# Reordering a kernel's start, its side jobs and the PSUM banks of its tail: attention plus token-mixing MLP on one core

## Chip, cores, metric

One core of a Trainium2 chip. The metric is the device time of one execution in microseconds (us), median of the executions. "Span" is the time from the first to the last profiled instruction; in these runs a timed execution is 1.7 us longer than its span. All comparisons are between executions of the fast state.

## The reference, cut to what matters

```python
xn = layernorm(x)                         # 2048 tokens x 1024
out = x + A(xn, wq, wk, wv, wo, beta) + B(xn, w1, b1, w2, b2)
# A: 32 heads of 32, 4 segments of 512 tokens: causal softmax attention inside a segment, plus
#    a linear-attention memory of the earlier segments, mixed by sigmoid(beta); then @ wo
# B: h = layernorm(xn); u = gelu(h^T w1 + b1) over tokens; y = u w2 + b2; transposed back
```

## The kernel before

One instruction stream per engine, written in program order by Python; semaphores are put in where data or PSUM banks are shared. It runs in four stages: the norm of the tokens with the first 512 hidden units (`h`, `w1early`), the rest of the MLP (a seven-product block scheme), 32 attention units (4 segments x 8 groups of 4 heads), and a tail. These parts are touched.

Names in the profile. `h` is a normed chunk of the MLP's input, `xs` the scaled tokens of a later segment. `kT` is the copy of the keys and `ost` that of the weighed values out of PSUM, the banks into which TensorE writes its products; a bank is free for the next product only when its copy is done. `pT` is the exp of the logits, on ScalarE. `srec`, `prod` and `o_s` scale a unit's output by its denominators and add its two parts; `fin` adds a product with `wo` to the output.

The start. `D`/`d` are a chunk's statistics on VectorE (a quote is the second half), `A` on ScalarE, `S` the reciprocal root (one VectorE and one GpSimd instruction), `h` the scaling that makes `h`:

```python
for kind, c0, n in (("x", 0, 1), ("x", 1, 1), ("x", 2, 1), ("w", 0, 2), ("x", 3, 1), ("x", 4, 2), ("w", 2, 2), ("x", 6, 2),
                    ("w", 4, 4), ("x", 8, 4), ("w", 8, 4), ("x", 12, 4), ("w", 12, 4)):
    ...                                   # one DMA each, chunks c0 to c0 + n of x or of w1's first 512 columns
for _ in range(self.N_WARM):              # N_WARM = 12
    fw.mm(self.bank(0), self.warm[:, 0:P], self.warm[:], start=True, stop=True)

NORM_ORDER = (["D0 A1 S0 d2 h0 A1' A3 S1 d2' h1"] +
              [f"S{c} d{c + 2} h{c} A{c + 1}' A{c + 3} S{c + 1} d{c + 2}' h{c + 1}" for c in range(2, 14, 2)] +
              ["S14 h14 A15' S15 C h15"])
```

The attention. TensorE's matmuls are cut into pieces (`dense`), and between the pieces one "side" job at a time is taken from a queue and emitted, mostly for VectorE. How many jobs a unit puts into the queue decides between which matmul pieces each of them falls, and so its place among VectorE's other instructions:

```python
def products(half):                       # combine(): scale a unit's outputs by their denominators
    n = slice(16 * half, 16 * half + 16)
    fw.op("dve", lambda e: e.tensor_tensor(self.prod[:, n, :], ost[:, n, 0:D_HEAD],
                                           rec[:, n].unsqueeze(2).to_broadcast([P, 16, D_HEAD]), op=ALU.mult), ...)
return [scales, lambda: products(0), lambda: products(1), add]        # four side jobs
...
# attention(), per unit u
c = 4 * (u // N_GRP + 1) + u % N_GRP
xn = u % N_GRP < 4 and c < N_TCH          # units 0-3, 8-11, 16-19 scale a chunk of the next segment's tokens
if xn:
    self.xn_load(c)
...
self.side.append(steps.pop(0))            # scales
self.side.append(lambda u=u: self.phi_q(u))
self.side.extend(steps)                   # products, products, add with the transposing DMA
self.side.append(lambda u=u: (self.phi_k(u + 1), self.k_transpose(u + 1)))
if xn:
    self.side.append(lambda c=c: (self.xn_scale(c), self.xn_transpose(c)))
```

`dense` jobs use PSUM banks 6 and 7 in turn, logits banks 0 to 3, the weighing of the values banks 4 and 5. The tail multiplies the last segment's output by `wo`:

```python
i, h, b = n // 2, n % 2, (6, 7, 0, 1, 2, 3, 5, 4)[n]      # bank of tail product n
```

The softmax here doesn't subtract the row's maximum and nothing guards it: scores larger than these inputs give would overflow.

Of the kernel before, what the change touches and what calls it, by code (L numbers as in the profile page):

```python
# [7 lines left out]
ALU = mybir.AluOpType  # L8
# [7 lines left out]
D_HEAD = 32  # L16
# [3 lines left out]
P = 128  # L20
N_TCH = S_TOK // P
# [8 lines left out]
N_GRP = N_HEAD // 4  # L30
# [354 lines left out]
class _Kernel:  # L385
    SB_BASE = 16512
    SB_END = 229344
    LEAD = 2
    N_WARM = 12
    G_AT = 3584  # L390
    B_AT = G_AT + 7 * 14336

# [104 lines left out]
    def consts(self):  # L497
        fw = self.fw
        fw.op("dve", lambda e: e.memset(self.warm[:], 0.0), writes=[self.R_warm])
        for brow, R in ((self.brow1, self.R_brow1), (self.brow2, self.R_brow2)):  # L500
            fw.op("dve", lambda e: e.memset(brow[:], 0.0), writes=[R[4]])
        self.w1_ring = _Ring(fw, [t[:] for t in self.w1s], self.R_w1s, depth=0)
        for fp in range(2, N_FCH // 2):
            self.w1_ring.srcs.append(self.B_w1[:, fp * 256:(fp + 1) * 256].rearrange("(c p) f -> p c f", p=P))
        fw.op("act", lambda e: e.activation(self.junk[:, 0:1], self.warm[:, 0:1], ACT.Gelu_apprx_tanh),
              reads=[self.R_warm], writes=[self.R_junk])
        for kind, c0, n in (("x", 0, 1), ("x", 1, 1), ("x", 2, 1), ("w", 0, 2), ("x", 3, 1), ("x", 4, 2), ("w", 2, 2), ("x", 6, 2),
                            ("w", 4, 4), ("x", 8, 4), ("w", 8, 4), ("x", 12, 4), ("w", 12, 4)):
            if kind == "x":
                self.load_x(c0, n)  # L510
            else:
                self.fw.dma(self.w1early[:, c0:c0 + n, :],
                            self.B_w1[c0 * P:(c0 + n) * P, 0:512].rearrange("(c p) f -> p c f", p=P),
                            writes=self.R_w1e[c0:c0 + n])
        for brow, src, n, R in ((self.brow1, self.B_b1, N_FCH, self.R_brow1), (self.brow2, self.B_b2, N_TCH, self.R_brow2)):
            for j in range(4):
                fw.dma(brow[32 * j:32 * j + n, :], src.rearrange("(c q) -> c q", q=P)[:, 32 * j:32 * j + 32],
                       reads=[R[4]], writes=[R[j]])
        fw.dma(self.beta[:], self.A_beta.partition_broadcast(P), writes=[self.R_beta])
        self.w1_ring.ensure(0)  # L520
        self.w1_ring.ensure(1)

        fw.op("pool", lambda e: e.memset(self.expo[:], -0.5), writes=[self.R_expo])
        fw.op("pool", lambda e: e.memset(self.ident[:], 0.0), writes=[self.R_ident])
        fw.op("pool", lambda e: e.affine_select(self.ident[:], self.ident[:], pattern=[[-1, P]],
                                                compare_op=ALU.not_equal, fill=1.0, base=0,
                                                channel_multiplier=1),
              reads=[self.R_ident], writes=[self.R_ident])
        with fw.group(reads=[self.R_warm], writes=[self.R_bank[0]]):
            for _ in range(self.N_WARM):  # L530
                fw.mm(self.bank(0), self.warm[:, 0:P], self.warm[:], start=True, stop=True)
# [13 lines left out]
    def gates(self):  # L545
# [12 lines left out]
        fw.op("dve", lambda e: e.tensor_copy(self.gate[:, :, 1, :], gv),  # L558
              reads=[self.R_gcol, self.R_gate], writes=[self.R_gate])

    NORM_ORDER = (["D0 A1 S0 d2 h0 A1' A3 S1 d2' h1"] +
                  [f"S{c} d{c + 2} h{c} A{c + 1}' A{c + 3} S{c + 1} d{c + 2}' h{c + 1}" for c in range(2, 14, 2)] +
                  ["S14 h14 A15' S15 C h15"])

    def norm_and_first_hidden(self):
        for word in " ".join(self.NORM_ORDER).split():
            kind, second = word[0], word.endswith("'")
            c = int(word[1:].rstrip("'") or 0)
            if kind == "C":
                self.bias_columns()  # L570
            elif kind in "Dd":
                self.stats_dve(c, (0, 1) if kind == "D" else (1,) if second else (0,))
            elif kind == "A":
                self.stats_act(c, second)
            elif kind == "S":
                self.rstd(c)
            else:
                self.scale_h(c)
        for c in range(N_TCH - 2):
            self.early_hidden(c, c + 1, (range(0, 8, 2), range(1, 8, 2)))  # L580
        self.early_hidden(N_TCH - 2, N_TCH, [(b,) for b in range(8)])
        self.rstd_first()
# [37 lines left out]
        fw.op("pool", lambda e: e.tensor_tensor(rs, rs, self.expo[:], op=ALU.pow), reads=[self.R_rs0, self.R_expo],  # L620
              writes=[self.R_rs0])

    def scale_h(self, c):
        reads = [self.R_xin[c], self.R_st[c], self.R_rs[c]]
        both = getattr(self, f"h_{c % 2}")
        for h0, h1 in ((0, 1), (1, 2)) if c < 2 else ((0, 2),):
            src = self.xin[:, c, 512 * h0:512 * h1].rearrange("p (d x) -> p d x", x=512)
            self.fw.op("dve", lambda e: e.tensor_scalar(both[:, h0:h1, c // 2, :], src, self.ln_mv[:, c, 0:1],
                                                        self.ln_rs[:, c, 1:2], op0=ALU.subtract, op1=ALU.mult),
                       reads=reads, writes=[self.R_h[c % 2][d][c // 2] for d in range(h0, h1)])  # L630
# [649 lines left out]
    def combine(self, u):  # L1280

        fw = self.fw
        s, g, o = u // N_GRP, u % N_GRP, u % 2
        ost, R_ost = self.ost[o], self.R_ost[o]
        rec, R_rec = self.srec[:, o, :], self.R_srec[o]
# [23 lines left out]
            fw.op("dve", lambda e: e.reciprocal(rec, rec), reads=[R_rec], writes=[R_rec])  # L1309
            fw.op("dve", lambda e: e.tensor_tensor(rv, rv, g8, op=ALU.mult), reads=[R_rec, self.R_gate], writes=[R_rec])  # L1310

        def products(half):
            n = slice(16 * half, 16 * half + 16)
            fw.op("dve", lambda e: e.tensor_tensor(self.prod[:, n, :], ost[:, n, 0:D_HEAD],  # L1314
                                                   rec[:, n].unsqueeze(2).to_broadcast([P, 16, D_HEAD]), op=ALU.mult),
                  reads=R_ost + [R_rec, self.R_prod], writes=[self.R_prod])

        def add():
            pv = self.prod[:].rearrange("p (q k r) d -> p q k (r d)", q=4, k=2)
# [2 lines left out]

        if s == 0:
            return [scales_first, products_first]
        return [scales, lambda: products(0), lambda: products(1), add]

    def o_transpose_dma(self, u):
        s, g, o = u // N_GRP, u % N_GRP, u % 2
# [12 lines left out]
              reads=[self.R_bank[b]], writes=[self.R_oT[s % 2][g]])  # L1341

    STOPS, STOPS_DVE = (1, 4, 7), (1, 4)

    def unit_jobs(self, u):
        jobs = [self.wo_job(*x) for x in self.wo_plan.get(u, ())]
# [7 lines left out]
    def attention(self):  # L1354
# [17 lines left out]
        for u in range(N_UNIT):  # L1372
            even = u % 2 == 0
            self.jobs.extend(self.unit_jobs(u))
            total = 8 * len(self.jobs) - sum(j[0] for j in self.jobs)
            c = 4 * (u // N_GRP + 1) + u % N_GRP
            xn = u % N_GRP < 4 and c < N_TCH
            if xn:
                self.xn_load(c)
            if u < 10:  # L1380
                cuts = self.cut(total, (0, 4, 2, 4, 1, 13, 8) if even else (7, 3, 2, 4, 1, 15))
            else:
                cuts = self.cut(total, (0, 4, 2, 2, 2, 14, 8) if even else (7, 3, 2, 2, 2, 16))
            end = u >= N_UNIT - 4
            self.dense(cuts[0])
            self.logits(u, 0)
            self.dense(cuts[1], end)
            while end and self.side:
                self.side.popleft()()
            if u:  # L1390
                self.weigh(u - 1, 0)
            self.dense(cuts[2], False)
            if u:
                self.weigh(u - 1, 1)
            self.dense(cuts[3], False)
            if u:
                self.weigh(u - 1, 2)
                steps = self.combine(u - 1)
                last = steps[-1]
                steps[-1] = lambda u=u, last=last: (last(), self.o_transpose_dma(u - 1))  # L1400
                self.side.append(steps.pop(0))
            if N_GRP <= u:
                self.side.append(lambda u=u: self.phi_q(u))
            if u:
                self.side.extend(steps)
            if u + 1 < N_UNIT:
                self.side.append(lambda u=u: (self.phi_k(u + 1), self.k_transpose(u + 1)))
            if xn:
                self.side.append(lambda c=c: (self.xn_scale(c), self.xn_transpose(c)))
            self.dense(cuts[4])  # L1410
            self.logits(u, 1)
            if even:
                self.dense(cuts[5])
                self.logits(u, 2)
            self.dense(100)
# [13 lines left out]
    def tail(self):  # L1429
        fw = self.fw  # L1430
        s, u = N_SEG - 1, N_UNIT - 1
# [2 lines left out]
            self.load_fin(4 * s + i)  # L1434

        def product(n, j0, j1, cols=((0, 512),)):
            i, h, b = n // 2, n % 2, (6, 7, 0, 1, 2, 3, 5, 4)[n]
            for p, (c0, c1) in enumerate(cols):
                with fw.group(reads=[self.R_wo] + self.R_oT[s % 2][j0:j1], writes=[self.R_bank[b]]):
                    for jc in range(j0, j1):  # L1440
# [2 lines left out]
                if j1 < N_GRP:  # L1443
# [5 lines left out]
                      reads=[self.R_bank[b], R], writes=[R])  # L1449
                fw.dma(self.out_d[:, 4 * s + i, h * 512 + c0:h * 512 + c1], dst, reads=[R],  # L1450
                       is_output=True, issuer=("sp", "act")[p % 2])
                b = (b + 1) % 3

        product(0, 0, 6)
        product(1, 0, 6)
        self.weigh(u, 0)
        self.weigh(u, 1)
# [43 lines left out]
```

## Time and profile before

| | |
|---|---|
| timed executions | 657.39, 657.58, 657.68 us |
| the profiled execution itself | span 657.9, time 659.62 us |
| TensorE busy | 648.8 us, 99% |

The busy times from part 1 of the profile page, and the stretches of the first 20 us (columns: stretch, length, busy time of PE, PEld, DVE, ACT and POOL with their instructions, then PEclk, the TensorE clock granted, DMA share, GB/s):

```profile
PE 648.8 (99%) x4624; PEld 303.1 (46%) x4624; DVE 426.7 (65%) x821; ACT 275.9 (42%) x297; POOL 146.6 (22%) x181
```

```profile
1.20:4.00 2.80, 2.75 (x7) 1.04 (x8) 0.52 (x3) 1.09 (x2) 0.29 (x1) 1.00 0.75 226
4.10:7.40 3.30, 1.27 (x6) 0.39 (x4) 2.26 (x7) 2.39 (x4) 0.55 (x1) 1.00 0.92 298
7.50:10.80 3.30, 3.30 (x8) 1.11 (x9) 3.22 (x11) 3.07 (x5) 1.26 (x3) 0.50 1.04 367
```

TensorE is full, so only places where it stands or runs slowly matter. From 4.1 to 7.4 us it works 1.27 of 3.3 us; in the next 3.3 us it is 100% busy, but with 8 matmuls at clock 0.50, where about 15 would fit. (The 1.00 of the first line is only the value ahead of the first recorded change: the matmuls there are 0.43 us apart, as slow as the 8.) The timeline of the start shows the hole: the warm-ups end at 5.4, the first product on `h` waits until 7.47.

```profile
1.25 4.12 PE L198 MATMUL ps_all<-warm 128*128 128x512 bf16 x12 [1.25 <-DVE brow L501]
...
6.93 0.72 DVE L628 TENSOR_SCALAR h<-xin,ln_mv,ln_rs 128x512 f16<-128x512 bf16 x2
...
7.47 5.70 PE L198 MATMUL ps_all<-h,w1early 128*128 128x512 f16 x18 [2.11 <-DVE h L628]
```

TensorE's list of waits (us in total, times, longest) and VectorE's timeline ahead of the longest wait in the attention, at 470.6 us. VectorE goes from one instruction to the next without a pause, and the copy of `kT` that TensorE needs (to get a PSUM bank back) is simply late in the line:

```profile
PE ps_all L198 <- DVE h L628: 2.1, 1, 2.1
PE ps_all L198 <- DVE brow L501: 1.2, 1, 1.2
PE ps_all L198 <- DVE fin L1158: 1.2, 1, 1.2
PE ps_all L198 <- DVE kT L1112: 0.9, 1, 0.9
PE ps_all L198 <- ACT pT L1216: 0.5, 2, 0.4
PE ps_all L198 <- DVE ost L1267: 0.3, 1, 0.3
```

```profile
467.16 1.42 DVE L1314 TENSOR_TENSOR prod<-ost,srec 128x512 bf16<-128x512 bf16 x2
468.61 0.43 DVE L1320 TENSOR_TENSOR o_s<-prod 128x512 bf16<-128x512 bf16 x1
468.95 0.72 DVE L1080 TENSOR_SCALAR mtmp<-etmp 128x512 bf16<-128x512 bf16 x1
469.71 1.00 DVE L1082 SCALAR_TENSOR_TENSOR mtmp<-kT,mtmp 128x512 bf16<-128x512 bf16 x1
470.63 0.68 DVE L1112 CAST kT<-ps_all 128x512 bf16<-128x512 f32 x1
```

The tail. The second product wants bank 7, and the last `fin` add has not read it yet:

```profile
640.23 0.68 DVE L1158 TENSOR_TENSOR fin<-ps_all,fin 128x512 bf16<-128x512 f32 x1
...
640.96 1.47 PE L198 MATMUL ps_all<-wo,oT 128*128 128x512 bf16 x6 [1.17 <-DVE fin L1158]
```

### The profile page before, as it was taken

Reading aid. Unit: us, or ns where it says so; the run is one execution under the profiler, and the core shown is the slowest. Engines: PE = TensorE matmul, PEld = TensorE weight load, DVE = VectorE, ACT = ScalarE, POOL = GpSimd, SP = SyncE. Lnnn points to the kernel's source line nnn. Section 1 sums busy time; section 2 is a strip of 40 time slices with the busy share of each in tenths; the row PEclk is TensorE's granted clock in tenths of the full one; section 3 lists DMA queues with packets and bytes.
Section 4 is the critical chain, followed back from the end, with each engine's and each line's share of the span. In section 5 each row is a group of like instructions: output and inputs, shape, how many; then the busy total and the mean of one; then the engine's idle time right before and its main releaser. Section 6 shows DMA issues by size and latency. Waiting matters only on the chain.

```text
span 657.9 us, 11118 instructions
## 1 busy us (share of the span) xinstructions
PE 648.8 (99%) x4624; PEld 303.1 (46%) x4624; DVE 426.7 (65%) x821; ACT 275.9 (42%) x297; POOL 146.6 (22%) x181
## 2 busy tenths in 40 slices
PE   7999999999999999999999999999999999999988
PEld 3444444444444444444444445554454554444444
DVE  6965676665644553344422476589888998877895
ACT  7542232232210000000011777887667766767750
POOL 2500000000011222022220243333233333333440
PEclk8999999999999999999999999999999999999999
DMA  8704233242556546854386586568644784445424
GB/s 305 208 0 129 65 93 100 64 115 78 132 172 179 153 122 170 181 156 117 96 220 200 152 174 132 104 155 160 130 94 116 176 171 116 118 97 83 80 81 137
DMA packets 187242, 87.65 MB, mean 133 GB/s; under 512 B 116024, under 2 KB 174392, under 8 KB 187192
## 3 DMA queue, kind: packets, MB, share of 16 engines
q1 hardware_dynamic: 187048, 86.91, 53.3%
q8 instruction: 36, 0.59, 0.4%
q14 instruction: 14, 0.11, 0.1%
q10 hardware_dynamic: 144, 0.03, 0.0%
HBM read 67.13 MB, written 8.39 MB: 115 GB/s over the span
## 4 chain that ended last, share of the span: by engine, by line
PE 92%; DVE 6%; issue 1%; DMA 1%; ACT 0%; SPq 0%; DVEq 0%
PE ps_all L198 92%; DVE prod L1314 1%; DVE fin L1158 1%; DMA xin<-in_A_x_dram 1%; DVE fin L1448 1%; DVE ost L1267 0%; DVE mtmp L1082 0%; DVE mtmp L1080 0%; DVE o_s L1320 0%; DVE pqT L1082 0%; ACT pT L1216 0%; DVE srec L1309 0%; DVE xs L986 0%; DVE kT L1112 0%; DVE srec L1308 0%
## 5 line engine op out<-in xcount | busy, mean ns | idle before, releaser
L1216 ACT ACTIVATE pT<-ps_all 128x2048 bf16<-128x2048 f32 x80 | 150.1, 1876 | 55.4 <-PE ps_all L198 55.3
L1220 POOL TENSOR_SCALAR_AFFINE_SELECT pT<-pT 128x512 bf16<-128x512 bf16 x128 | 98.1, 783 | 195.5 <-ACT pT L1216 195.5
L690 DVE TENSOR_TENSOR part<-ps_all,part 128x512 f32<-128x512 f32 x76 | 52.5, 691 | 119.0 <-PE ps_all L198 118.2
L926 POOL TENSOR_TENSOR part<-part,stg 128x512 f32<-128x512 f32 x24 | 33.0, 1401 | 266.2 <-DVE part L690 266.2
L695 ACT ACTIVATE part<-ps_all 128x512 f32<-128x512 f32 x20 | 11.9, 597 | 149.0 <-PE ps_all L198 149.0
L198 PE MATMUL ps_all<-wv,xnT 128*128 128x512 bf16 x256 | 68.5, 380 | 0.9 <-DVE kT L1112 0.9
L742 ACT ACTIVATE g<-part,b1c 128x512 f16<-128x512 f32 x36 | 26.0, 722 | 98.9 <-DVE part L690 98.9
L198 PE MATMUL ps_all<-wo,oT 128*128 128x512 bf16 (+2 forms) x272 | 65.8, 367 | 1.2 <-DVE fin L1158 1.2
L198 PE MATMUL ps_all<-xnT,wq 128*128 128x512 bf16 x256 | 63.6, 380 | 0.0
L198 PE MATMUL ps_all<-xnT,wk 128*128 128x512 bf16 x256 | 61.8, 380 | 0.0
L1267 DVE CAST ost<-ps_all 128x396 bf16<-128x396 f32 (+2 forms) x96 | 44.6, 475 | 25.3 <-PE ps_all L198 24.0
L198 PEld LDWEIGHTS ps_all<-vA,pT 128*128 128x128 bf16 x1280 | 45.4, 96 | 20.4 <-DVE ost L1267 3.9
L198 PE MATMUL ps_all<-g,w2s 128*128 128x512 f16 x224 | 51.0, 379 | 0.0
L198 PE MATMUL ps_all<-g,sum 128*128 128x512 f16 x224 | 51.0, 379 | 0.0
L198 PE MATMUL ps_all<-gT,sum 128*128 128x512 f16 x224 | 49.7, 379 | 0.0
L198 PE MATMUL ps_all<-vA,pT 128*128 128x33 bf16 x1280 | 48.6, 178 | 0.4 <-DVE ost L1267 0.3
L198 PE MATMUL ps_all<-h,sum 128*128 128x512 f16 x192 | 45.2, 379 | 0.0
L198 PE MATMUL ps_all<-h,w1s 128*128 128x512 f16 x192 | 44.9, 379 | 0.0
L198 PE MATMUL ps_all<-hT,sum 128*128 128x512 f16 x192 | 43.6, 379 | 0.0
L1314 DVE TENSOR_TENSOR prod<-ost,srec 128x512 bf16<-128x512 bf16 x48 | 40.9, 852 | 0.8
L198 PEld LDWEIGHTS ps_all<-xnT,wk 128*128 128x128 bf16 x256 | 23.8, 98 | 29.8 <-issue 3.2
L198 PEld LDWEIGHTS ps_all<-wo,oT 128*128 128x128 bf16 x272 | 23.5, 97 | 25.9 <-issue 5.4
(99 smaller groups left out, 804.5 us busy)
## 6 DMA issues: line engine op xcount, KB each, us to landing
w2s<-in_B_w_dram SPq DMA_DIRECT2D x8, 1792.0 KB, 8.6
w1s<-in_B_w_dram SPq DMA_DIRECT2D x12, 1024.0 KB, 5.6
wq<-in_A_wq_dram SPq DMA_DIRECT2D x32, 256.0 KB, 3.3
wk<-in_A_wk_dram SPq DMA_DIRECT2D x32, 256.0 KB, 3.3
stg<-in_A_x_dram SPq DMA_DIRECT2D x16, 256.0 KB, 3.0
xs<-in_A_x_dram SPq DMA_DIRECT2D x16, 256.0 KB, 3.4
out_dram<-stg SPq DMA_DIRECT2D x16, 256.0 KB, 2.9
fin<-out_dram SPq DMA_DIRECT2D x16, 256.0 KB, 3.6
```

The lines of the kernel that those rows point to most:

```text
L198: ins = self.nc.tensor.matmul(*args, **kwargs)
L690: self.fw.op("dve", lambda e: e.tensor_tensor(self.tmp[dst][:], self.bank(b), self.tmp[src][:], op=ALU.add), reads=[self.R_bank[b], self.R ...
L695: self.fw.op("act", lambda e: e.activation(self.tmp[dst][:], self.bank(b), ACT.Copy), reads=[self.R_bank[b]], writes=[self.R_tmp[dst]])
L742: self.fw.op("act", lambda e: e.activation(self.gB[f % 2][half][:, f // 2, :], src, ACT.Gelu_apprx_tanh, bias=self.b1c[:, f:f + 1], scale= ...
L926: fw.op("pool", lambda e: e.tensor_tensor(self.tmp[t][:], self.tmp[t][:], self.stg[k][:, 512 * half:512 * half + 512], op=ALU.add), reads= ...
L1158: self.fw.op("dve", lambda e: e.tensor_tensor(dst, self.bank(b), dst.bitcast(F16), op=ALU.add), reads=[self.R_bank[b], R], writes=[R])
L1216: fw.op("act", lambda e: e.activation(dst, src, ACT.Exp, scale=SCALE), reads=self.R_bank[0:4], writes=[R[v % 2][kb] for v, kb, _ in blocks ...
L1220: fw.op("pool", lambda e: e.affine_select(d, d, pattern=[[0, 4], [1, P]], compare_op=ALU.is_ge, fill=0.0, base=0, channel_multiplier=-1), ...
L1267: fw.op("dve", lambda e: e.tensor_copy(dst, src), reads=[self.R_bank[b]], writes=[self.R_ost[o][part]])
L1314: fw.op("dve", lambda e: e.tensor_tensor(self.prod[:, n, :], ost[:, n, 0:D_HEAD], rec[:, n].unsqueeze(2).to_broadcast([P, 16, D_HEAD]), op ...
L1448: fw.op("dve", lambda e: e.tensor_tensor(dst, self.ps[:, b, c0:c1], dst.bitcast(F16), op=ALU.add), reads=[self.R_bank[b], R], writes=[R])
```

## The change

The intent: the first product sooner and no hole that cools the clock (h0 ahead of the third chunk's statistics, h0 and h1 in halves, w1's first two chunks as two DMAs, 15 warm-ups); VectorE shorter in the attention (one `prod` instruction for two) and its token scaling two units earlier for the last two segments; no bank wait in the tail.

```diff
-    N_WARM = 12
+    N_WARM = 15
@@ loads
-... ("x", 2, 1), ("w", 0, 2), ("x", 3, 1), ("x", 4, 2), ("w", 2, 2), ("x", 6, 2),
+... ("x", 2, 1), ("w", 0, 1), ("x", 3, 1), ("w", 1, 1), ("x", 4, 2), ("w", 2, 2), ("x", 6, 2),
@@ order of the norm
-    NORM_ORDER = (["D0 A1 S0 d2 h0 A1' A3 S1 d2' h1"] +
-                  [f"S{c} d{c + 2} h{c} ..." for c in range(2, 14, 2)] +
+    NORM_ORDER = (["D0 A1 A1' A3 S0 h0 h0' S1 d2 h1 d2' S2 h1' h2 d4 A3' A5 S3 d4' h3"] +
+                  [f"S{c} d{c + 2} h{c} ..." for c in range(4, 14, 2)] +
-                self.scale_h(c)
+                self.scale_h(c, ((0, 2),) if c > 1 else ((1, 2),) if second else ((0, 1),))
@@ combine
-        def products(half):
-            n = slice(16 * half, 16 * half + 16)
-            ... self.prod[:, n, :], ost[:, n, 0:D_HEAD], rec[:, n] ... [P, 16, D_HEAD]
+        def products():
+            ... self.prod[:], ost[:, :, 0:D_HEAD], rec ... [P, 32, D_HEAD]
-        return [scales, lambda: products(0), lambda: products(1), add]
+        return [scales, products, add]
@@ attention
+    XN_AT = (0, 1, 2, 3, 6, 7, 8, 9, 14, 15, 16, 17)
-            c = 4 * (u // N_GRP + 1) + u % N_GRP
-            xn = u % N_GRP < 4 and c < N_TCH
-            if xn:
-                self.xn_load(c)
+            xn = self.XN_AT.index(u) + 4 if u in self.XN_AT else None
+            if u in self.XN_AT[::4]:
+                self.xn_load(xn)
+                self.xn_load(xn + 1)
-                self.side.append(lambda c=c: (self.xn_scale(c), self.xn_transpose(c)))
+                self.side.append(lambda c=xn: (self.xn_scale(c), self.xn_transpose(c), c % 4 < 2 and self.xn_load(c + 2)))
@@ tail
-            i, h, b = n // 2, n % 2, (6, 7, 0, 1, 2, 3, 5, 4)[n]
+            i, h, b = n // 2, n % 2, (0, 1, 2, 3, 6, 7, 5, 4)[n]
```

More of the change, by code (lines that the diff above doesn't have):

```diff
@@ L506, in consts @@
               reads=[self.R_warm], writes=[self.R_junk])
-        for kind, c0, n in (("x", 0, 1), ("x", 1, 1), ("x", 2, 1), ("w", 0, 2), ("x", 3, 1), ("x", 4, 2), ("w", 2, 2), ("x", 6, 2),
+        for kind, c0, n in (("x", 0, 1), ("x", 1, 1), ("x", 2, 1), ("w", 0, 1), ("x", 3, 1), ("w", 1, 1), ("x", 4, 2), ("w", 2, 2), ("x", 6, 2),
                             ("w", 4, 4), ("x", 8, 4), ("w", 8, 4), ("x", 12, 4), ("w", 12, 4)):
@@ L559, in gates @@
               reads=[self.R_gcol, self.R_gate], writes=[self.R_gate])
-    NORM_ORDER = (["D0 A1 S0 d2 h0 A1' A3 S1 d2' h1"] +
-                  [f"S{c} d{c + 2} h{c} A{c + 1}' A{c + 3} S{c + 1} d{c + 2}' h{c + 1}" for c in range(2, 14, 2)] +
+    NORM_ORDER = (["D0 A1 A1' A3 S0 h0 h0' S1 d2 h1 d2' S2 h1' h2 d4 A3' A5 S3 d4' h3"] +
+                  [f"S{c} d{c + 2} h{c} A{c + 1}' A{c + 3} S{c + 1} d{c + 2}' h{c + 1}" for c in range(4, 14, 2)] +
                   ["S14 h14 A15' S15 C h15"])
@@ L621, in rstd_first, with scale_h @@
               writes=[self.R_rs0])
-    def scale_h(self, c):
+    def scale_h(self, c, parts):
         reads = [self.R_xin[c], self.R_st[c], self.R_rs[c]]
         both = getattr(self, f"h_{c % 2}")
-        for h0, h1 in ((0, 1), (1, 2)) if c < 2 else ((0, 2),):
+        for h0, h1 in parts:
             src = self.xin[:, c, 512 * h0:512 * h1].rearrange("p (d x) -> p d x", x=512)
@@ L1310, in scales @@
             fw.op("dve", lambda e: e.tensor_tensor(rv, rv, g8, op=ALU.mult), reads=[R_rec, self.R_gate], writes=[R_rec])
-        def products(half):
-            n = slice(16 * half, 16 * half + 16)
-            fw.op("dve", lambda e: e.tensor_tensor(self.prod[:, n, :], ost[:, n, 0:D_HEAD],
-                                                   rec[:, n].unsqueeze(2).to_broadcast([P, 16, D_HEAD]), op=ALU.mult),
-                  reads=R_ost + [R_rec, self.R_prod], writes=[self.R_prod])
+        def products():
+            fw.op("dve", lambda e: e.tensor_tensor(self.prod[:], ost[:, :, 0:D_HEAD],
+                                                   rec.unsqueeze(2).to_broadcast([P, 32, D_HEAD]), op=ALU.mult),
+                  reads=R_ost + [R_rec], writes=[self.R_prod])
         def add():
@@ L1407, in attention @@
                 self.side.append(lambda u=u: (self.phi_k(u + 1), self.k_transpose(u + 1)))
-            if xn:
-                self.side.append(lambda c=c: (self.xn_scale(c), self.xn_transpose(c)))
+            if xn is not None:
+                self.side.append(lambda c=xn: (self.xn_scale(c), self.xn_transpose(c), c % 4 < 2 and self.xn_load(c + 2)))
             self.dense(cuts[4])
```

## The prediction

> **What bounds it.** TensorE. The page gives it 648.8 of 657.9 us busy, and the chain that ended last is 92% its matmuls. Only four places leave it short:
>
> - Start. By the timeline the 12 warm-up matmuls end about 5.3 us, and the first product on `h` starts at 7.47: 2.1 us idle, put down to `h`; the weight load before it to the `w1early` DMA (landed about 7.0). The granted clock is full from about 4.0 to 7.4, but half from 7.4 to 10.8, so the first 8 products start 0.43 us apart instead of 0.216: 1.7 us lost.
> - 450 to 471 us (attention, units 9 to 11): VectorE is behind; TensorE waits 0.9 us for the `kT` copy at 470, about 0.4 us for `kT`/`ost` at 451 to 453.
> - 619 to 634 us: 0.2 and 0.4 us on `ost`, 0.5 us on the exp (`pT`).
> - 639.6 us: the second tail product needs bank 7, still being read by the `fin` add: 1.2 us (list of waits; 1.3 by start-to-start spacing).
>
> **What the change does.**
>
> 1. Start. `h0` no longer queues behind the third chunk's statistics, whose data landed at 6.3. The reciprocal root ends at 6.0, so half of `h0` (0.36 us) is ready at about 6.5; chunk 0 of `w1`, now half the bytes, should land at about 6.6 (estimate: half of the 0.67 us between the landings before and now). First product about 6.7, 0.75 us sooner. Three more warm-ups at 0.216 us end at about 5.9, so the hole shrinks to 0.8 us. The Trainium skill ("TensorE: Matmul & The Clock Gate", Part 1) describes a free-running 3.4 us activity window that throttles an idle array; this trace agrees (steps 3.41 us apart). A window about a third busy was throttled here; holes of 0.9 and 1.2 us later were not. I expect the clock to stay full: 1.7 us. But `h` then becomes the limit: statistics of chunk 2 are delayed, and I estimate stalls of 0.1 us before the second half of `h1`, 0.1 before `h2`, 0.4 before `h3` (ready about 12.4, against 11.8 now). Net 1.8 us.
> 2. `prod` in one instruction instead of two: two of 128x512 take 1.42 us undisturbed, 1.7 to 2.2 beside POOL. I estimate 0.15 to 0.3 us saved per unit. Off the critical path except where VectorE is behind, and in the tail's chain (0.34 us hole at 648.3, about 0.16 us recovered).
> 3. Token scaling (0.54 us each) moves from units 8-11 and 16-19 to 6-9 and 14-17. Units 10 and 11 lose it, so the 470 wait should mostly go: 0.9 us; with item 2 about half of the smaller `kT`/`ost` waits, 0.5 us.
> 4. Tail in banks 0 and 1: their last reader, the exp, ends about 637.7, before 639.6. Wait gone: 1.3 us.
>
> **Sum.** 1.8 + 0.9 + 0.5 + 1.3 + 0.15 = 4.65; minus 0.2 for new small waits: 4.5 us, so 653.1 us. 80% range 651.3 to 655.4. Faster by over 2%: 1%; within 2%: 98%; slower: 1%.
>
> **What would show it.** Granted clock full from about 4 us on; first product at 6.7; small waits on `h` before 13 us; no `fin` wait in the tail; `kT` wait at 470 gone; 24 `prod` instructions of 128x1024.
>
> **What would make it wrong.** The window's phase: if 0.8 us idle still counts as idle, 1.7 us stay lost (655). Larger `h` stalls for chunks 1 to 3. A later-landing `w1` chunk. The earlier token transposes blocking the SP queue and delaying weights or `pk`, giving new waits in units 6 to 9.

## The result, and the profile after

The changed kernel takes 655.84 us (655.65 to 655.92, 4 executions), the kernel before 657.63 (medians): ratio 0.9974, 95% interval 0.9954 to 0.9993. A ratio here is the mean time of one kernel's fast runs over the mean of the other's of the same rounds, so not quite the ratio of the medians quoted beside it. Executions over 1.5% slower than the fastest of the same kernel are left out of the means. 1.8 us were gained where 4.5 were forecast, and the upper end of the forecast was 655.4.

The two profiled spans tell another story: 657.9 and 654.1, a gain of 3.8 us. The difference between 3.8 and 1.8 was the first thing to explain.

The same views as before:

```profile
PE 642.6 (98%) x4572; PEld 303.4 (46%) x4627; DVE 422.5 (65%) x797; ACT 276.1 (42%) x297; POOL 152.9 (23%) x181
```

```profile
4.10:7.40 3.30, 2.91 (x13) 1.11 (x12) 2.45 (x8) 2.95 (x5) 0.93 (x2) 1.00 0.99 292
7.50:10.80 3.30, 3.00 (x14) 0.99 (x11) 2.57 (x8) 2.26 (x5) 0.73 (x2) 1.00 1.02 358
```

```profile
1.25 5.06 PE L198 MATMUL ps_all<-warm 128*128 128x512 bf16 x15 [1.25 <-DVE brow L501]
6.15 0.73 DVE L628 TENSOR_SCALAR h<-xin,ln_mv,ln_rs 128x512 f16<-128x512 bf16 x2 [0.75 <-POOL ln_rs L612]
6.71 3.84 PE L198 MATMUL ps_all<-h,w1early 128*128 128x512 f16 x16 [0.39 <-DVE h L628]
...
11.01 2.33 PE L198 MATMUL ps_all<-h,w1early 128*128 128x512 f16 x10 [0.46 <-DMA w1early<-in_B_w_dram]
12.01 0.49 DVE L628 TENSOR_SCALAR h<-xin,ln_mv,ln_rs 128x1024 f16<-128x1024 bf16 x1
```

The first product starts at 6.71, as forecast. This trace records no change of the clock, so its 1.00 shows nothing; that the products run at full clock is read from their spacing, 0.216 us. In the three other traces with the same start (e2, e7, e13) the first product starts at 7.24, 6.80 and 7.04: where the 15 warm-ups run at half clock for longer, they end later. Then the third chunk of `w1` keeps it waiting at 11.0, and `h3` ends at 12.5 (11.8 before). TensorE's waits:

```profile
PE ps_all L198 <- issue: 2.7, 17, 0.2
PE ps_all L198 <- DVE brow L501: 1.3, 1, 1.3
PE ps_all L198 <- DVE ost L1267: 0.5, 2, 0.3
PE ps_all L198 <- ACT pT L1216: 0.5, 2, 0.4
PE ps_all L198 <- DMA w1early<-in_B_w_dram: 0.5, 1, 0.5
```

The `kT` and `fin` waits are gone. "issue", 17 times 0.16 us, is no wait: 55 matmul records are missing in this trace (4572 of 4627), and a missing one can leave a gap; e13, the same kernel with all 4627 records, has none of these. So PE busy must not be compared between these two traces. I compare stages by anchors that are complete in all traces, the 80 exp instructions of the attention (stage = from the first exp to the 80th; tail = from there to the end). The two waits on `ost` are new; here is the first. TensorE starts again at 498.02, after the first of the two `ost` copies, which ended at 497.97 (the third part of the weighing uses the same bank, 4, as the first), and ahead of `kT` and the copies VectorE has scaled tokens (`xs`):

```profile
496.35 0.54 DVE L986 TENSOR_SCALAR xs<-xs,ln_mv,ln_rs 128x1024 bf16<-128x1024 bf16 x1
496.80 0.69 DVE L1112 CAST kT<-ps_all 128x512 bf16<-128x512 f32 x1
497.40 1.04 DVE L1267 CAST ost<-ps_all 128x396 bf16<-128x396 f32 x2
```

```profile
498.02 0.57 PE L198 MATMUL ps_all<-vA,pT 128*128 128x33 bf16 x16 [0.26 <-DVE ost L1267]
```

In the tail the products follow one another, since banks 0 and 1 were last read by the exp that ended at 635.3:

```profile
633.27 5.35 PE L198 MATMUL ps_all<-wo,oT 128*128 128x512 bf16 x24
633.32 0.35 DVE L1309 RECIPROCAL srec<-srec 128x32 f32<-128x32 f32 x1
633.39 1.88 ACT L1216 ACTIVATE pT<-ps_all 128x2048 bf16<-128x2048 f32 x1 [1.53 <-PE ps_all L198]
```

### The profile page after: what moved, and what is told of

The parts are those of the page before. It is cut to its first block, busy times and chain, and to the rows that moved or that the text cites. A ratio compares the mean times of both kernels' runs of the same rounds, so it can differ in the third digit from the quotient of the medians.

```text
span 654.1 us, 11050 instructions
## 1 busy us (share of the span) xinstructions
PE 642.6 (98%) x4572; PEld 303.4 (46%) x4627; DVE 422.5 (65%) x797; ACT 276.1 (42%) x297; POOL 152.9 (23%) x181
## 4 chain that ended last, share of the span: by engine, by line
PE 92%; DVE 4%; issue 1%; DMA 1%; ACT 1%; SPq 0%; DVEq 0%
PE ps_all L198 92%; DMA w1early<-in_B_w_dram 1%; ACT pT L1216 1%; DVE fin L1448 1%; DVE prod L1313 1%; DVE ost L1267 1%; DVE mtmp L1080 0%; DVE mtmp L1082 0%; SPq L220 0%; DVE fin L1158 0%; DVE kT L1112 0%; DVE xs L986 0%; DVE srec L1309 0%; DVE MZbf L1277 0%; DVE pqT L1082 0%
## 5 line engine op out<-in xcount | busy, mean ns | idle before, releaser
L1220 POOL TENSOR_SCALAR_AFFINE_SELECT pT<-pT 128x512 bf16<-128x512 bf16 x128 | 104.1, 831 | 189.0 <-ACT pT L1216 188.8
L198 PE MATMUL ps_all<-wv,xnT 128*128 128x512 bf16 x238 | 64.6, 379 | 1.8 <-issue 0.6
L198 PE MATMUL ps_all<-wo,oT 128*128 128x512 bf16 (+2 forms) x254 | 61.0, 366 | 1.1 <-issue 0.6
L198 PE MATMUL ps_all<-xnT,wq 128*128 128x512 bf16 x248 | 61.2, 380 | 0.2
L198 PE MATMUL ps_all<-xnT,wk 128*128 128x512 bf16 x245 | 59.6, 379 | 1.5 <-issue 1.4
L198 PEld LDWEIGHTS ps_all<-xnT,wq 128*128 128x128 bf16 x256 | 22.8, 97 | 26.9 <-issue 4.6
```

What stands on the lines that cost most here:

```text
L198: ins = self.nc.tensor.matmul(*args, **kwargs)
L1220: fw.op("pool", lambda e: e.affine_select(d, d, pattern=[[0, 4], [1, P]], compare_op=ALU.is_ge, fill=0.0, base=0, channel_multiplier=-1), ...
```

## The experiments

Theory A: the profiled execution of before was an unusual one, and ordinary executions never had the half-clock stretch; so the 1.7 us were not there to be gained. Rival B: every execution of before has it, the gain at the start is real, and it was lost again later. Fifteen runs were made, 5 rounds each except e5 and e6 (one look). All gave correct results. The stage columns are from the profiled execution, in us: start of the first exp (the start and the MLP), first to last exp (attention), last exp to end (tail).

| run | what it is | time | ratio to before | first exp | attention | tail |
|---|---|---|---|---|---|---|
| first trace | before | 659.62 | | 365.49 | 270.37 | 22.03 |
| e1 | before | 657.62 | 1.0004 | 363.94 | 270.34 | 22.01 |
| e2 | + start part | 657.84 | 1.0003 | 363.74 | 270.35 | 22.03 |
| e3 | + tail banks | 656.41 | 0.9979 | 363.64 | 270.36 | 20.68 |
| e4 | + prod + scaling | 656.45 | 0.9981 | 363.31 | 269.59 | 21.50 |
| e5 | + prod | 656.54 | | 363.26 | 270.05 | 21.50 |
| e6 | + scaling | 656.60 | | 363.42 | 269.42 | 22.02 |
| after | all | 655.84 | 0.9974 | 363.80 | 269.59 | 20.67 |
| e7 | after, last segment scaled in 16-19 | 655.72 | 0.9970 | 363.61 | 269.60 | 20.68 |
| e8 | after, start of before | 655.36 | 0.9964 | 363.46 | 269.59 | 20.67 |
| e9 | before, 6 warm-ups | 659.88 | 1.0027 | 365.79 | 270.37 | 22.02 |
| e10 | scaling + tail + prod only at the end | 655.08 | 0.9961 | 363.57 | 269.13 | 20.65 |
| e11 | e10, another start | 655.33 | 0.9966 | 363.78 | 269.20 | 20.67 |
| e12 | before, order of the norm only | 657.85 | 1.0006 | 363.68 | 270.36 | 22.02 |
| e13 | after | 655.78 | 0.9976 | 364.07 | 269.58 | 20.66 |
| e14 | e15 with an empty job | 654.44 | 0.9954 | 364.19 | 268.41 | 20.67 |
| e15 | after, start of before | 655.61 | 0.9971 | slow | slow | slow |

Attention and tail repeat to 0.05 us wherever the instructions are the same, so a difference of 0.1 us in these columns means something. The first exp does not repeat: among kernels with the start of before at full clock it ranges over 0.9 us (363.26 to 364.19).

### e1: before, unchanged

> The kernel before, unchanged, timed against itself. Theory A (the clock): its ordinary executions run at full granted clock (clock 1.000, span about 655.8, time about 657.5), and the profiled one of the first trace (span 657.9, clock 0.997, time 659.6) was the odd one, with 3.4 us at half clock after the warm-up hole. Then clock and time go together: any execution near 659.5 shows 0.997. Rival B (the later stages): every execution has the half-clock stretch, clock 0.997 throughout, and the 659.6 of the profiled one is the profiler's cost; the gain at the start was then real and was lost again in the attention. Ratio 1.000 under both.

The five executions took 657.28 to 659.61. The one of 659.61 has span 657.9 and mean clock 0.997; the others 1.000. Of the kernel before's executions in the four calls and at the outset (45 with a usable time), three took 659.6 us or more, each with clock 0.997: the first profiled one, this one, and one of 659.76 in the last call. The profile of e1 happens to be an ordinary one. The array wakes 1.7 us later than in the first trace (at 5.76 instead of 4.02), so the 12 warm-ups run cold and last until 6.2, and the hole before the first product is 0.6 us and not 2.1:

```profile
1.25 4.97 PE L198 MATMUL ps_all<-warm 128*128 128x512 bf16 x12 [1.25 <-DVE brow L501]
6.30 0.72 DVE L628 TENSOR_SCALAR h<-xin,ln_mv,ln_rs 128x512 f16<-128x512 bf16 x2
6.85 3.63 PE L198 MATMUL ps_all<-h,w1early 128*128 128x512 f16 x16 [0.62 <-DMA w1early<-in_B_w_dram]
```

`h0` is also 0.6 us earlier here, with the old order: the data of the third chunk landed at 5.67 instead of 6.29, so its statistics were not in the way. Theory A holds; the execution of 659.61 was not the profiled one, so the profiler's cost does not explain it.

### e2: the start part alone

```diff
+ N_WARM = 15, w1 chunks 0 and 1 as two DMAs, the new NORM_ORDER, h0 and h1 in halves
```

> Before plus only the start part (order of the norm, h in halves, w1 split, 15 warm-ups). Theory A: at full clock on both sides the 0.75 us earlier start is eaten by 0.9 us of waits on h and w1 for chunks 1 to 3: 657.3 to 657.9 us, ratio 0.9995 to 1.0005; clock 1.000. Rival B: the half-clock stretch goes, 1.6 us less: about 656.0, ratio 0.9975.

657.84, as theory A said, and steady (657.83 to 658.03). The start part gains nothing against an ordinary execution of before. Whether it removes the rare slow start is not shown: none of the 19 executions with this start (e2, after, e7, e13) was slow, but at 3 in 45 only about one would be expected. In its trace all 15 warm-ups ran cold and ended at 7.4, so they delayed the first product to 7.24.

### e3: the tail's banks alone

> Before plus only the other banks in the tail. Both theories: the 1.2 us wait of the second tail product on the fin add goes, nothing else: 656.2 to 656.5 us, ratio 0.9980 (1.3 us).

656.41, ratio 0.9979; the tail shrank from 22.02 to 20.68. As expected.

### e4: prod and token scaling

> Before plus only the middle part (one prod instruction, token scaling two units earlier). From the two traces: the 1.0 us wait on kT near 471 goes, two new waits of 0.4 us on ost near 500 and 519 come, 0.2 to 0.3 us less at 630: net 0.5 to 0.8 us less, 656.8 to 657.1, ratio 0.9990. Rival B needs a loss of over 1 us here: 658.5 or more, ratio 1.0015.

656.45, a little better than expected, and not the loss that rival B needed. The attention gained 0.75 us, and the tail another 0.5, since the shorter `prod` lets the `fin` add come sooner. That half microsecond is the same time that the other banks win, so it is not had twice: with the other banks the tail is 20.67 with one instruction and 20.68 with two.

### e5 and e6: one prod instruction; the scaling moved

```diff
e5: -        return [scales, lambda: products(0), lambda: products(1), add]
    +        return [scales, products, add]
e6: +    XN_AT = (0, 1, 2, 3, 6, 7, 8, 9, 14, 15, 16, 17)      # and the loads that go with it
```

> Before plus only the one prod instruction. Read in the trace against e3's middle (same instructions as before), by the start of each exp. Theory P: merging is what shortens VectorE's queue, so the 1.2 us kT wait near 470 shrinks to under 0.3 us here. Theory X: moving the token scaling out of units 10 and 11 is what does it, so over 0.7 us of the wait stays here. The two new ost waits of 0.39 us near 498 and 517 should be absent, if they come from the moved scaling. Tail: fin wait 1.2 us becomes 0.7 us, as in e4.

> Before plus only the earlier token scaling. Theory X: the kT wait near 470 is gone (under 0.2 us) and the two ost waits near 498 and 517 are here, 0.4 us each. Theory P: the kT wait keeps at least 0.9 us. If the ost waits are in neither e5 nor e6, they need both parts (a missing job moves the scaling one place ahead in the queue). Fin wait in the tail stays 1.2 us.

Each alone removes the `kT` wait near 470, so neither P (the merging) nor X (the moved scaling) was right as the only cause. From TensorE's waits of e5, then of e6:

```profile
PE ps_all L198 <- DVE ost L1267: 0.8, 3, 0.3
```

```profile
PE ps_all L198 <- DVE ost L1267: 0.3, 1, 0.3
PE ps_all L198 <- DVE kT L1112: 0.2, 1, 0.2
```

The one `ost` wait of e6 is the old one near 631, and its `kT` wait stands at 506. The new `ost` waits belong to e5, not to the moved scaling as I had thought. In e5 they stand at 459.6, 516.9 and 536.2, each 1.7 us after a token scaling starts (457.95, 515.18, 534.54); in the changed kernel at 498.0 and 517.4, again 1.7 us after one (496.35, 515.71). By the exps (how much later the next exp comes than in e3) each costs 0.39 us in the changed kernel, and the three of e5 cost 0.44, 0.39 and 0.40. So e5 wins 1.0 us at 470 and 0.5 in small steps elsewhere (0.24 of it at 633) and gives back 1.2: 0.3 net. e6 wins the 1.0 at 470 alone and keeps 0.93. The `fin` wait is 0.7 us in e5 and 1.2 in e6, as expected.

### e7: the last segment's tokens at their old units

```diff
- XN_AT = (..., 14, 15, 16, 17)
+ XN_AT = (..., 16, 17, 18, 19)
```

> The changed kernel, but the last segment's tokens scaled in units 16 to 19 as before. If the early place in units 14 to 17 makes the two ost waits, they go: 0.8 us less than the changed kernel, span 653.3, time about 655.0. If VectorE is just as late wherever the scaling sits, the waits move to units 16 to 20 and the time stays 655.8.

655.72 and an attention of 269.60: the second branch. The waits moved, to 516.8 and 536.1; they were not removed.

### e8: the changed kernel without its start part

> The changed kernel with the start of before (order, undivided w1 load, 12 warm-ups). Theory A (the start part is worth nothing at full clock): 655.2 to 655.9 with a spread of 1 us, against 655.8 of the changed kernel, and about one execution in ten 2 us slower with clock 0.997. Rival B (the start part is worth 1.6 us): 657.4.

655.36 (655.14 to 655.69). No execution of the five was a slow one. The start part was not worth 1.6 us, against rival B.

### e9: a hole on purpose

```diff
- N_WARM = 12
+ N_WARM = 6
```

> Before with 6 warm-ups instead of 12, so that the hole ahead of the first product is 3 us in every execution. Theory A (a window mostly idle throttles the array, and that alone made the first trace 2 us slower): first products 0.43 us apart, clock 0.997 or a little less, all executions near 659.3, 1.7 us above before (ratio 1.0026). Against it: the products run 0.216 us apart and the time stays 657.5, or the time rises with the clock at 1.000.

659.88 (658.55 to 660.07), ratio 1.0027:

```profile
1.25 2.74 PE L198 MATMUL ps_all<-warm 128*128 128x512 bf16 x6 [1.25 <-DVE brow L501]
7.21 5.96 PE L198 MATMUL ps_all<-h,w1early 128*128 128x512 f16 x16 [3.22 <-DVE ln_mv L610]
```

In the trace the first product comes at 7.21 after 3.2 us of idling, and the first eleven are 0.40 to 0.43 us apart. So a cold array at the first products costs 0.9 to 2.4 us against the median of before, 2.2 in the medians. In this trace the six warm-ups are 0.40 to 0.43 us apart too: the array had not woken yet, so the trace shows what cold products cost, and not that a hole cools a warm array. That is recorded in the first trace alone (full from 4.02, half from 7.43). My expectation about the mean clock was wrong, though: three of these five executions, among them the profiled one, are listed with clock 1.000. The profiled one's trace records no change of the clock at all, so the mean of a run can miss a cold start; the spacing of the matmuls cannot.

### e10: two products in the attention, one at the end

```diff
+        if u >= N_UNIT - 5:
+            return [scales, products_whole, add]
         return [scales, lambda: products(0), lambda: products(1), add]
```

> Before plus earlier token scaling plus the tail's banks, with the one prod instruction only in the last five units, and the start as before. If the ost waits come from the merged prod (e5: three of 0.39 us; e6: none), the attention has neither the kT wait nor ost waits: 0.3 to 0.45 us less than e8, 654.9 to 655.1. If it is the late stages that make the difference: 655.4 as e8.

655.08, no `ost` wait, the attention 0.46 us shorter than e8's. As expected.

### e11 and e12: the start again

```diff
e11: loads   x0 x1 w0 x2 w1 x3 w2-3 x4-5 x6-7 ...
     order   ... S2 h1' A3' A5 h2 S3 d4 h3 d4' ...        N_WARM = 13
e12: only the new NORM_ORDER and the halves; loads and 12 warm-ups as before
```

> e10 with another start: h0 early and in halves, w1 chunks ahead of the x chunks that come later, the root and scaling of chunk 3 ahead of the statistics of chunk 4, 13 warm-ups. If the h3 chain is what set the changed kernel's start (h3 ready at 12.5 against 11.2 to 12.1 in the old order), h3 is now ready by 11.9 and the fifth chunk's products start near 13.7 instead of 14.1 to 14.4: 0.3 us less than e10, 654.6 to 654.8. If landings set it, no gain: 655.0 or more.

> Before with the new order of the norm alone (w1 load undivided, 12 warm-ups). If the order is what makes the start part 0.3 us slower at full clock: h3 ends at 12.5, the fifth chunk's products start at 14.3 to 14.4, 657.8 as e2. If the divided load (later landing of x4, x5 and w1 chunks 2, 3) does it: h3 before 12.2, fifth chunk at 14.0, 657.5.

| kernel | first product | h0 half ends (two) | h2 ends | h3 ends | h4 ends | fifth chunk's products |
|---|---|---|---|---|---|---|
| first trace (before) | 7.47 | 7.33, 7.65 | 10.50 | 11.81 | 13.15 | 16.03 |
| e4 (old start, best) | 6.85 | 6.71, 7.03 | 9.90 | 11.24 | 12.58 | 13.76 |
| e8 (old start) | 7.06 | 6.91, 7.23 | 10.54 | 11.88 | 13.23 | 14.14 |
| after | 6.71 | 6.56, 6.88 | 10.52 | 12.51 | 13.85 | 14.47 |
| e12 (new order only) | 6.66 | 6.51, 6.83 | 10.47 | 12.45 | 13.79 | 14.24 |
| e11 | 6.61 | 6.47, 6.79 | 10.42 | 11.85 | 14.17 | 14.31 |

(us, from the traces.) e11 failed: `h3` came at 11.85 as planned, but `h4` slipped to 14.17 and became the wait instead. e12 shows that the order alone makes `h3` end at 12.45. Whatever comes first by 0.3 us is lost by the fourth or fifth chunk. In the traces of after and e12 VectorE stands idle for 0.5 us just ahead of `h2`, until GpSimd has made chunk 2's root; so `h2` comes no earlier (10.5 in both, 10.46 in the mean of the old starts), though `d4` is no longer ahead of it. From there VectorE has no pause up to `h3`, and both statistics of chunk 4 (0.69 us each) now stand between `h2` and `h3`, where the old order has one. The row of e4 is the best of the old starts and not a typical one: over the eight full-clock traces with the old start (e1, e3 to e6, e8, e10, e14) the fifth chunk's products start at 14.17 in the mean (13.76 to 14.64), over the four with the new one at 14.36 (14.28 to 14.47). The times of e2 and e12 (657.84, 657.85) are not told apart from before by their intervals.

### e13, e14, e15: what the merged prod does, and the start once more

```diff
e14, against e15:
-        return [scales, products, add]
+        return [scales, products, lambda: None, add]
```

> The changed kernel, beside e14 and e15 on one chip. 655.8, as first measured; the fifth chunk's products start at 14.3 to 14.5, two ost waits of 0.26 us idle near 498 and 517.

> e15 with an empty job in place of the second product, so the order of VectorE is e10's, with one long instruction instead of two. Theory O (order): no ost waits, 655.0, 0.4 us less than e15. Theory L (the long instruction): the waits of 0.39 us stay, 655.4.

> The changed kernel with the start of before. If the start part costs 0.3 us at full clock: 655.4, 0.3 to 0.5 us under e13. If the difference of e8 was the chip's: within 0.1 us of e13.

e14 took 654.44 us (653.87 to 655.15), the best of all: ratio 0.9954 to before. It has the same instructions as e15; the empty job only keeps the queue at its old length, so that the scaling falls behind the `ost` copies again. No `ost` wait is left, and the attention takes 268.41 us, 1.18 less than with the shorter queue. The same place in its timeline:

```profile
496.42 0.68 DVE L1112 CAST kT<-ps_all 128x512 bf16<-128x512 f32 x1
497.02 1.04 DVE L1267 CAST ost<-ps_all 128x396 bf16<-128x396 f32 x2
497.97 0.68 DVE L1158 TENSOR_TENSOR fin<-ps_all,fin 128x512 bf16<-128x512 f32 x1
498.57 0.43 DVE L1267 CAST ost<-ps_all 128x264 bf16<-128x264 f32 x1
...
499.44 0.54 DVE L986 TENSOR_SCALAR xs<-xs,ln_mv,ln_rs 128x1024 bf16<-128x1024 bf16 x1
```

So theory O: the order did it, not the longer instruction. The gain was three times what I had expected (0.4 us): by the exps the two places of the `ost` waits give 0.87 us of the 1.18, and 0.32 comes near 454, where `kT` is now copied ahead of `o_s` and `mtmp`. Nor is the merging useless: e10, with two products and no `ost` wait either, takes 269.13, so in the right order one instruction is worth another 0.7 us. e13 repeated at 655.78 (655.69 to 656.04), e15's four fast executions lie at 655.28 to 655.64 beside it: the start part costs 0.2 us by the medians and 0.3 by the means here, less than e8 had suggested. The profiled execution of e15 fell in the slow state, so its trace is not used.

## Why the prediction was wrong, point by point

What each stage gave, on the columns of the table (before at full clock against after; the first exp as the mean of e1, e3, e4, e5, e6, e8, e10, e14 against that of e2, after, e7, e13):

| term | predicted | measured |
|---|---|---|
| start | 1.8 | 363.60 - 363.81 = -0.2 |
| `kT` wait near 470 | 0.9 | 1.0 |
| small `kT`/`ost` waits, items 2 and 3 | 0.5 | 0.5 |
| new small waits | -0.2 | -0.8 |
| tail, with the 0.15 of `prod` | 1.45 | 22.02 - 20.67 = 1.35 |
| sum | 4.5 | 1.9 (timed: 1.8) |

- **The step that failed is item 1, "I expect the clock to stay full: 1.7 us ... Net 1.8 us."** The clock did stay full. But it is full in ordinary executions of before too; only about one in fifteen (3 of 45) has the half-clock stretch, and the trace that I costed was one of them. e1 shows it; e2 and e8 show that adding or removing the start part changes the time by 0.5 us at most, where the forecast needed 1.8; and e9 shows that cold first products cost 2.2 us when nearly every execution has them. What put the first trace into its phase is not shown. The sign was on the page from the start: the profiled execution took 659.62 us while the timed ones took 657.4 to 657.7. The forecast subtracted savings read from the slow execution from the median of the fast ones.
- The rest of item 1 was right in its parts and of no use in the sum. The first product at 6.7, the smaller hole and the later `h3` came as forecast (predicted ready at 12.4, measured 12.5), the first two in the profiled execution of the changed kernel and not in all: in e2 and e13 the first product came at 7.24 and 7.04. But in ordinary executions the old order starts at 6.8 to 7.4 as well, and the later `h3` takes back what is left. The Trainium skill ("TensorE: Matmul & The Clock Gate", Part 1) says of the windows that they are free-running and that the same kernel can measure a different number of cold matmuls at each start. The recorded changes to full clock, at 4.02, 4.66, 4.68, 5.13, 5.27, 5.55, 5.76, 5.95, 6.42, 6.52, 6.67 and 6.84 us in different traces, agree; I had named this phase as a risk for the changed kernel and not thought of it for the kernel before.
- Item 3 was right: the `kT` wait went, worth 1.0 us. The units were named wrongly: side jobs run behind their unit, and by the exps the wait stands in unit 13, after the scaling that ran in unit 12. The merged `prod` alone would have removed it too (e5).
- Item 2 was right about VectorE's time: its busy time falls from 426.7 to 422.5 us over 24 units, about 0.18 us each, where 0.15 to 0.3 was forecast. (An undisturbed pair takes 684 + 691 ns, one instruction 1218. The Trainium skill ("VectorE: DVE Perf Modes", Side-by-side section) breaks an instruction down with an init of about 150 cycles, an estimate of 156 ns at its 0.96 GHz, which fits the 157 ns saved. 23 of the 48 halves took 1.0 us or more, so all of `prod` fell by 10.8 us; but the `mtmp` and `o_s` instructions became longer by 6.) It was wrong about its effect. In the tail it recovered nothing once the banks were changed. In the attention it won the 0.5 us of small waits (e5 has them, e6 does not), but the shorter queue moved the scaling ahead of the `ost` copies: two new waits of 0.39 us, where I had allowed 0.2 in all. I looked for new waits in the DMA queue of units 6 to 9 and not in VectorE's order, where `xs` now stands ahead of `kT` and `ost` in two places (496.35 and 515.71).
- Item 4 was right: 1.35 us, in e3 alone and in the whole.

Left open: whether the start part's 0.2 us loss is one at all. The timed medians of e2, e8, e13 and e15 and the fifth chunk's products all point that way, but the first exp of the old start varies by 0.9 us, as it seems with the landing of the first DMAs. The start part ran on two of the chips used in the experiments (e2 and e7 on chip 2, e13 on chip 11); no run set the phase of the clock.

## What to carry to other kernels

Before costing a trace, compare the profiled execution's own time with the timed ones; if they differ by as much as the expected gain, find out what that execution had that the others have not. When work is handed out by position in a queue, removing an instruction moves its neighbours: keep the place with an empty job, and look at the new order of the engine that is behind, not only at its sum of busy time. In a start where several chunks queue for one engine, bringing the first result forward is worth only what the later results do not lose.

## What the Trainium skill lacked or had wrong

- "TensorE: Matmul & The Clock Gate", HAM oscillation section: gives the rule of no idle gaps over about 3.4 us. Here a gap of 2.1 us throttled: TensorE worked 1.27 of 3.3 us in that window, and the next window ran at clock 0.50, with 8 matmuls 0.43 us apart. Gaps of 0.9 and 1.2 us did not throttle, nor did one of 1.64 us in e10, whose products follow at 0.216 us.
- The same page, Part 1, calls the cold start's count run-variable and its penalty under 1% of a typical kernel. True here (2 us of 657), but it is as large as the change being measured; the page does not say how rare a phase can be, nor that the profiled execution can be in the rarer one (3 of 45 of before's).
- The same page's caveat on clock records warns that the events are unreliable; it does not say that a run's mean clock can miss the cold start. Three executions of e9 of 658.6 to 660.1 us are listed at 1.000, and the trace of one has eleven products at 0.40 to 0.43 us.
- No page that I used has the spread of the landing of the same first loads: the third `xin` chunk landed at 5.29 to 6.29 us and `w1early`'s first two at 6.38 to 7.18 in the eleven traces of kernels with the same loads (first trace, e1, e3 to e6, e8 to e10, e12, e14; the slow one of e15 left out).
